# Lightning attention and an ELU expert on one core: block 1's keys and values in fp32 from another queue, one product of GpSimd moved, and fifteen products that nothing reads

## The chip, the core and the metric

The kernel runs on one core of a Trainium2 chip. The metric is the device time of one execution, in microseconds; 2% counts as a difference in the verdicts.

## The reference

Two stages, fp32 in and out.

Attention with decay, for 4 batches and 8 heads, 768 positions in 12 blocks of 64, head size 64. In each block, with a state per head that starts at zero:

```
intra = ((q k^T) * lam^(i-j), where i >= j) v
inter = (q * lam^(i+1)) state
out   = intra + inter
state = lam^64 * state + (k * lam^(63-j))^T v
```

The output, 3072 tokens of 512 features, then goes through `h = x @ w_in` (512 to 2048), `g = h if h > 0 else exp(h) - 1`, and `g @ w_out` (2048 to 512).

## The kernel before, in words

The four batches make two pairs; a "block" of the kernel is one block of 64 positions of both batches of a pair, 128 rows, so there are 24 of them (`NS`), numbered so that block 0 is the first of pair 0 and block 1 the first of pair 1. Two blocks make a group of 256 tokens (`grp`, 12 of them).

The order of the work is written out by hand: each engine executes its instructions in the order in which the program emits them. For the first blocks the order is the string `start`, of words such as `V1` (a letter for a step, a number for a block); the rest is a loop over groups and over eight units `u` of each.

The steps of a block: keys, queries and values are loaded and cast to fp16 (`load`, line 79; the queries of the first blocks at line 76) by GpSimd's DMA queue, which casts on the way. `visit(so, us, ss, sx)` (word `A`) is TensorE's work on up to four blocks: the output of block `so` (lines 337 and 346), the state product of `us` (353), the scores of `ss` (361), the transposes of `sx` (404 for queries, 409 for keys). Around it: `V` is `decay_v` (line 205, tile vd, the values scaled by the tile rev), `C` is `att_C` (251 and 252, the transposes copied out of PSUM into T), `P` the masked scores (240), `Q` is `decay_q` (232, tile qs, the queries scaled by powi), `D` is `decay_s` (223, tile sd, the decayed state), `N` the new state (293 and 297, tile st), `X` the copy of a block's output into xt (281). `K1` computes lamL and powi on ScalarE (608, 610); `F` casts block 0's fp32 keys and queries (193). From block 10 on the transposes come from a DMA (`dma_T`, tile TD), and `decay_q` runs on GpSimd.

The second stage: `H` is a unit of mm1 (line 434, PSUM tile psH, two buffers), `E` and `G` its ELU (444, 446 on ScalarE, 451 on VectorE; in the later loop 478, 480 and 481), `M` a part of mm2 (501), `Z` its copy and store (508, 510). In the loop mm2 is done as seven half-size products per group (557) on sums and differences `s` of parts of g (539) and `wt` of w_out.

The loads before the change, all on GpSimd's queue in this order: block 0's values, block 1's keys, queries and values, the first quarter of w_in (`wi[0]`, two transfers, line 97), block 2, `wi[1]`, block 3, `wi[2]`, `wo[0]` (a quarter of w_out, line 105), `wi[3]`, `wo[1]`, `wo[2]`, block 4, `wo[3]`, and so on. Block 0's keys come in fp32 on the sync queue SP (line 121), its queries in fp32 on ScalarE's queue (line 118). GpSimd has eight semaphores for its transfers, taken in turn: an issue waits until the transfer eight issues earlier has landed. In the loop, two loads of a later block are issued in units 0 and 4 of a group, and `decay_q` of the next block in unit 1 or 5.

Of the kernel before, what the change touches and what calls it, by code (L numbers as in the profile page):

```python
# [8 lines left out]
FP32 = mybir.dt.float32  # L9
FP16 = mybir.dt.float16  # L10
# [6 lines left out]
def kernel(  # L17
# [10 lines left out]
    nc = tc.nc  # L28

    B, H, S, D = q.shape  # L30
    L = 64
# [21 lines left out]
    def half(x):  # L53
        return slice(64 * x, 64 * x + 64)
# [5 lines left out]
    NB = 12  # L60
# [6 lines left out]
    def eights(b, c):  # L67

        return q[b : b + 2, :, c * L : (c + 1) * L, :].rearrange("r h (p g) d -> (r h) p (g d)", g=8)
# [14 lines left out]
    def load_step(s):  # L84
        load("k", s)
        load("q", s)
        load("v", s)
# [23 lines left out]
    for r in range(2):  # L111
        nc.gpsimd.iota(ij[half(r)], pattern=[[1, L]], base=0, channel_multiplier=-1)

    raw0 = {}
    for which, src in (("k", k), ("q", q)):
        raw0[which] = inp.tile([128, H, D], FP32, name=f"{which}raw0")
        if which == "q":
            nc.scalar.dma_start(out=raw0[which][:].rearrange("p h d -> p (h d)"), in_=eights(0, 0))
            continue
        for r in range(2):  # L120
            nc.sync.dma_start(
                out=raw0[which][half(r)], in_=src[r, :, 0:L, :].rearrange("h p d -> p h d")
            )
    load("v", 0)
    load_step(1)
    load_wi(0)
    load_step(2)
    load_wi(1)
# [60 lines left out]
    def cast0(which):  # L189

        keep, tag = {"k": (kn, "kn"), "q": (qn, "qn")}[which]
        keep[0] = inp.tile([128, H, D], FP16, tag=tag, bufs=NB, name=f"{tag}0")
        nc.vector.tensor_copy(keep[0][:], raw0[which][:])


    Z = ps.tile([128, 2, 512], FP32, tag="z", name="psZ")
    psS = Z[:, :, 0 : NHP * L]
# [3 lines left out]
    def decay_v(s, eng):  # L201
        if s >= NS - NPR:
            return
        st[s]["vd"] = asb.tile([128, H, D], FP16, tag="vd", bufs=3, name=f"vd{s}")
        eng.tensor_tensor(  # L205
            out=st[s]["vd"][:], in0=vn[s][:],
            in1=rev[:].unsqueeze(2).broadcast_to([128, H, D]), op=ALU.mult,
        )

# [32 lines left out]
            in1=mask[:].rearrange("p y j t -> p y (j t)"), op=ALU.mult,  # L242
        )

    def att_C(s):
        if s >= NT:
            return
        T = asb.tile([128, 2, NHP, 2, L], FP16, tag="T", bufs=4, name=f"T{s}")
        psT = st[s].pop("psT")
        if s < NQ:  # L250
            nc.vector.tensor_copy(T[:, 0].rearrange("p j r t -> p (j r t)"), psT[0])
            nc.scalar.copy(
                out=T[:, 1].rearrange("p j r (t g) -> p (j r t) g", g=8),
                in_=psT[1].rearrange("p (g x) -> p x g", g=8),
            )
        else:
            nc.vector.tensor_copy(
                T[:].rearrange("p i j r t -> p r (i j) t"),
                psT.rearrange("p r (x t) -> p r x t", t=L),
            )  # L260
        st[s]["T"] = T
# [12 lines left out]
    def att_X(s, eng):  # L274
        g, hf = divmod(s, 2)
        if g not in xt:
            xt[g] = asb.tile([128, NHP, 256], FP16, tag="xt", bufs=3, name=f"xt{g}")
        to = xt[g][:, :, hf * 128 : (hf + 1) * 128].rearrange("p y (r t) -> p r y t", r=2)
        O = st[s].pop("O").rearrange("p r (y t) -> p r y t", y=NHP)
        if eng is nc.scalar:  # L280
            nc.scalar.copy(out=to, in_=O)  # L281
        else:
            eng.tensor_copy(to, O)
# [134 lines left out]

    gel = {}
    unit = {}  # L420
    NF2 = NFT // 2

    def features(nb, n0, step):
# [79 lines left out]
                start=(n == 0), stop=(n == NFT - 1),  # L503
            )

    def mm2_o(s):
        o = msb.tile([128, DM], FP32, tag="o", bufs=4, name=f"o{s}")
        nc.scalar.copy(out=o[:], in_=acc.pop(s))
        for r in range(2):
            nc.sync.dma_start(out=rows(s, r), in_=o[half(r), :])  # L510

# [89 lines left out]
    def consts(i):  # L601
# [10 lines left out]


    start = (
# [14 lines left out]
    steps = {  # L629
        "C": att_C, "P": att_P, "X": lambda s: att_X(s, nc.scalar),  # L630
        "Y": lambda s: att_X(s, nc.vector), "N": att_N, "D": lambda s: decay_s(s, eng=nc.vector), "L": load_step,
        "V": lambda s: decay_v(s, nc.vector if s < 99 else nc.gpsimd),
        "Q": lambda s: decay_q(s, nc.vector if s < 10 else nc.gpsimd),
        "H": mm1_h, "E": mm1_e, "G": mm1_g, "M": mm2, "Z": mm2_o, "K": consts, "B": w_sum, "T": dma_T,
    }
    for word in start.split():
        if word[0] == "A":
            visit(*(int(x) if x else None for x in word[1:].split(".")))
        elif word[0] == "F":
            cast0(word[1])  # L640
        else:
            steps[word[0]](*(int(x) for x in word[1:].split(".") if x))

# [6 lines left out]
    for grp in range(3, NG):  # L650
        old, new = grp - 2, grp - 1
        for u in range(8):
            mm1_h(grp, 0, 2, u, NF2)
            s = 2 * grp + 2 + u // 4
            if s < NS and u % 4 == 0:

                if nload < NS:
                    load("k", nload)
                    load("q", nload)
                if nload <= NS:  # L660
                    load("v", nload - 1)
                    nload += 1
            if s < NS and u % 4 == 1:
                if s != 10:
                    decay_q(s + 1, nc.vector if s < 10 else nc.gpsimd)
                if s not in (10, 11, 12):
                    decay_s(s + 1, eng=nc.vector if s < 10 else nc.gpsimd)
                visit(
                    s, s if s < NS - NPR else None, s + 1 if s + 1 < NS else None,
                    s + 2 if s + 2 < NT else None,  # L670
                )
                dma_T(s + 3)

            if (grp, u) in five:
                mm2(5, 4 * five.index((grp, u)))
            end = grp == NG - 1
            if old >= 3 and u in (0, 2):
                part(old, {0: 3, 2: 7}[u])
            if new >= 3:
                at_u = {1: 2, 3: 4, 4: 1, 5: 5, 6: 6, 7: 3} if end else {3: 2, 4: 1, 5: 4, 6: 5, 7: 6}  # L680
                if u in at_u:
                    part(new, at_u[u])

            if old >= 3 and u == 1:
                add(old, 0, hi, res[old]["A"][:, hi], "p35")
                store(2 * old, res[old][0], slice(0, DM))
            if old >= 3 and u == 0:
                g_sum(old, 3)
            if new >= 3 and u in (4, 5, 6):
                g_sum(new, {4: 1, 5: 2, 6: 4}[u])  # L690
            if end and u == 3:
                g_sum(new, 3)
            if new >= 3 and u == 4:
                add(new, 0, lo, res[new]["A"][:, hi], "p2")
            if s + 1 < NS:
                if u % 4 == 1:
                    att_P(s + 1)
                if u % 4 == 2:
                    att_C(s + 2)
                    att_N(s)  # L700
                if u in (3, 7) and grp > 3:
                    decay_v(s + 1, nc.vector)
                if (grp, u) == (4, 2):
                    decay_q(s + 1, nc.vector)
            if old >= 3 and u == 2:
                c2(old)
            if (grp, u) == (5, 0):
                w_sum(3, 1)
            elu(grp, u)
            if (grp, u) == (4, 4):  # L710
                decay_s(11)
            if (grp, u) in ((5, 2), (5, 4)):
                decay_s(13, range(2) if u == 2 else range(2, NHP))
            if grp == 3 and u in (3, 6):
                decay_v(s + 1, nc.vector)
            if s < NS and u % 4 == 1:
                att_X(s, nc.scalar)
            if (grp, u) == (4, 5):
                decay_s(12)
            if old >= 3 and u == 0:  # L720
                keep(old, "p35", res[old]["B"][:, hi])
            if new >= 3 and u == (1 if end else 3):
                keep(new, "p2", res[new]["B"][:, lo])
            if new >= 3 and u == (5 if end else 6):
                keep(new, "c45", res[new]["B"][:])
            if end and u == 6:
                keep(new, "u2", res[new]["A"][:, hi], 1)
            if end and u == 7:
                add(new, 0, hi, res[new]["B"][:, hi], "u2")
                store(2 * new, res[new][0], slice(0, DM))  # L730
            if (grp, u) == five[-1]:
                mm2_o(5)
# [58 lines left out]
```

## Time and profile before

| | |
|---|---|
| three runs | 206.19, 206.64, 209.43 us; median 206.64 |
| the profiled execution | 207.57 us |
| its span, first to last instruction | 205.8 us |
| ScalarE (ACT) busy | 146.4 us |
| GpSimd (POOL) busy, its DMA issues included | 122.4 us |
| DMA | 94258 packets, 24.36 MB |
| issues of keys by GpSimd (kn, x46) | 64.0 KB each, 4.5 us to landing |
| issues of w_in (wi, x8) | 256.0 KB each, 6.5 us to landing |

PE is TensorE, PEld its weight loads, DVE VectorE, ACT ScalarE, POOL GpSimd, SP the sync queue. In a line of the timeline stand the start and the length in us, engine, line of the kernel, operation, tiles written and read, shapes and count; in brackets the idle time of the engine ahead of it and what the profile holds to have ended it. In the page's rows of slices each digit is the busy share of a fortieth of the span in tenths. The DMA rows give packets, MB, and the time that the packets took as a share of 16 engines' time (packets overlap, so it can pass 100%).

### The profile page before, as it was taken

Reading aid. Unit: us, or ns where it says so; the run is one execution under the profiler, and the core shown is the slowest. Engines: PE = TensorE matmul, PEld = TensorE weight load, DVE = VectorE, ACT = ScalarE, POOL = GpSimd, SP = SyncE. Lnnn points to the kernel's source line nnn. Section 1 sums busy time; section 2 is a strip of 40 time slices with the busy share of each in tenths; the row PEclk is TensorE's granted clock in tenths of the full one; section 3 lists DMA queues with packets and bytes.
Section 4 is the critical chain, followed back from the end, with each engine's and each line's share of the span. In section 5 each row is a group of like instructions: output and inputs, shape, how many; then the busy total and the mean of one; then the engine's idle time right before and its main releaser. Section 6 shows DMA issues by size and latency. Waiting matters only on the chain.

```text
span 205.8 us, 7718 instructions
## 1 busy us (share of the span) xinstructions
PE 190.1 (92%) x3280; PEld 158.0 (77%) x3280; DVE 165.9 (81%) x278; ACT 146.4 (71%) x283; POOL 122.4 (59%) x173
## 2 busy tenths in 40 slices
PE   0679799999999999989999999999999999999991
PEld 0457678747776777878888888888888888888880
DVE  4677786779989898999988988979979866658671
ACT  5435786834783888997978878788688788876720
POOL 8986642899799779796978978978222200000000
PEclk9999999999999999999999999999999999999999
DMA  6999999999999999999799999999814204003043
GB/s 102 164 170 173 166 206 190 177 115 175 108 136 160 163 126 130 155 110 128 108 152 108 169 103 118 156 102 127 137 25 102 54 5 102 5 21 84 0 102 102
DMA packets 94258, 24.36 MB, mean 118 GB/s; under 512 B 86160, under 2 KB 91152, under 8 KB 94224
## 3 DMA queue, kind: packets, MB, share of 16 engines
q0 software_dynamic: 73648, 13.38, 92.6%
q1 hardware_dynamic: 20128, 10.03, 27.8%
q10 hardware_dynamic: 448, 0.46, 1.0%
q8 instruction: 25, 0.41, 0.9%
q14 instruction: 9, 0.07, 0.1%
HBM read 27.27 MB, written 6.29 MB: 163 GB/s over the span
## 4 chain that ended last, share of the span: by engine, by line
PE 85%; DVE 5%; POOL 3%; DMA 3%; issue 1%; ACT 1%; DVEq 0%; POOLq 0%; ACTq 0%
PE psH L434 40%; PE psM L557 22%; PE psM L501 10%; DMA wi<-in_moe_w_in_dram 3%; PE psO_None L337 2%; PE psZ L361 2%; POOL vn L79 1%; PE psO_None L346 1%; PE psHB L557 1%; PE psHA L557 1%; DVE g L451 1%; PE psZ L353 1%; DVE s L539 1%; DVE vd L205 1%; POOL kn L79 1%
## 5 line engine op out<-in xcount | busy, mean ns | idle before, releaser
L434 PE MATMUL psH<-xt,wi 128*128 128x256 f16 (+1 forms) x960 | 100.3, 254 | 2.7 <-issue 1.0
L434 PEld LDWEIGHTS <-wi 128*128 128x128 f16 x960 | 79.5, 99 | 13.3 <-issue 2.5
L481 DVE SCALAR_TENSOR_TENSOR g<-e,psH 128x512 f16<-128x512 f32 x58 | 39.8, 686 | 16.7 <-ACT e L480 16.2
L478 ACT ACTIVATE r<-psH 128x512 f32<-128x512 f32 x58 | 34.7, 599 | 18.3 <-PE psH L434 18.2
L480 ACT ACTIVATE e<-r 128x512 f32<-128x512 f32 x58 | 36.5, 630 | 1.9
L79 POOL DMA_DIRECT2D kn<-in_k_dram x46 | 32.3, 723 | 6.7 <-DMA wo<-in_moe_w_out_dram 3.6
L79 POOL DMA_DIRECT2D vn<-in_v_dram x48 | 33.8, 731 | 3.5 <-DMA wo<-in_moe_w_out_dram 2.0
L444 ACT ACTIVATE e<-psH 128x512 f32<-128x512 f32 x38 | 22.8, 599 | 16.3 <-PE psH L434 15.8
L557 PEld LDWEIGHTS <-s 128*128 128x128 f16 x288 | 28.1, 98 | 3.3
L451 DVE SCALAR_TENSOR_TENSOR g<-e,r 128x512 f16<-128x512 f32 x38 | 25.9, 687 | 4.9 <-ACT r L446 4.8
L79 POOL DMA_DIRECT2D qn<-in_q_dram x36 | 25.4, 736 | 1.4 <-DMA kn<-in_k_dram 0.9
L557 PE MATMUL psM<-wt,s 128*128 128x256 f16 x192 | 24.9, 273 | 0.0
L501 PE MATMUL psM<-wo,g 128*128 128x512 f16 x96 | 23.9, 379 | 0.0
L232 POOL TENSOR_TENSOR qs<-TD,powi 128x512 f16<-128x512 f16 x12 | 14.6, 1215 | 15.4 <-PE psO_None L337 13.7
L446 ACT ACTIVATE r<-psH 128x512 f16<-128x512 f32 x38 | 22.7, 598 | 0.0
L557 PEld LDWEIGHTS <-g 128*128 128x128 f16 x216 | 20.6, 98 | 2.6
L240 DVE TENSOR_TENSOR P<-psZ,mask 128x512 f16<-128x512 f32 x24 | 16.5, 687 | 1.8 <-PE psZ L361 1.4
L557 PE MATMUL psM<-wo,g 128*128 128x256 f16 x136 | 17.6, 273 | 0.0
L205 DVE TENSOR_TENSOR vd<-vn,rev 128x512 f16<-128x512 f16 x22 | 16.0, 729 | 0.1
L293 DVE TENSOR_TENSOR st<-psZ,sd 128x512 f16<-128x512 f32 x20 | 13.7, 684 | 1.0 <-PE psZ L353 0.9
L501 PEld LDWEIGHTS <-g 128*128 128x128 f16 x96 | 8.6, 98 | 7.1
L281 ACT CAST xt<-psO_None 128x512 f16<-128x512 f32 x20 | 11.6, 579 | 3.1 <-PE psO_None L346 3.1
(84 smaller groups left out, 214.1 us busy)
## 6 DMA issues: line engine op xcount, KB each, us to landing
out_dram<-o SPq DMA_DIRECT2D x45, 128.0 KB, 3.6
vn<-in_v_dram POOLq DMA_DIRECT2D x48, 64.0 KB, 5.0
kn<-in_k_dram POOLq DMA_DIRECT2D x46, 64.0 KB, 4.5
qn<-in_q_dram POOLq DMA_DIRECT2D x36, 64.0 KB, 4.4
wi<-in_moe_w_in_dram POOLq DMA_DIRECT2D x8, 256.0 KB, 6.5
wo<-in_moe_w_out_dram POOLq DMA_DIRECT2D x4, 512.0 KB, 11.7
qn<-in_q_dram POOLq DMA_DIRECT2D x5, 128.0 KB, 5.5
kraw<-in_k_dram SPq DMA_DIRECT2D x2, 128.0 KB, 4.8
```

Source lines behind the costliest of these rows:

```text
L79: nc.gpsimd.dma_start(out=keep[s][half(r)], in_=src[b + r, :, c * L : (c + 1) * L, :].rearrange("h p d -> p h d"),)
L205: eng.tensor_tensor(out=st[s]["vd"][:], in0=vn[s][:], in1=rev[:].unsqueeze(2).broadcast_to([128, H, D]), op=ALU.mult,)
L240: nc.vector.tensor_tensor(out=d["P"][:].rearrange("p y j t -> p y (j t)"), in0=psS, in1=mask[:].rearrange("p y j t -> p y (j t)"), op=ALU. ...
L434: nc.tensor.matmul(psH[:, i, :], lhsT=wi[n // 4][:, kk, (n % 4) * 128 : (n % 4 + 1) * 128], rhs=xt[grp][:, kk, c0 * 128 : c0 * 128 + T], s ...
L444: nc.scalar.activation(e[:], psH[:], AF.Exp)
L446: nc.scalar.activation(r[:], psH[:], AF.Relu)
L451: nc.vector.scalar_tensor_tensor(out=place(grp, c0, nc_, n0, nb, step), in0=e[:], scalar=-1.0, in1=r[:], op0=ALU.add, op1=ALU.min,)
L478: nc.scalar.activation(r[:], psH[:], AF.Relu, scale=-1.0)
L480: nc.scalar.activation(e[:], r[:], AF.Exp, scale=-1.0)
L481: nc.vector.scalar_tensor_tensor(out=place(grp, 0, 2, u, 2, NF2), in0=e[:], scalar=-1.0, in1=psH[:], op0=ALU.add, op1=ALU.max,)
L501: nc.tensor.matmul(acc[s], lhsT=g_of(s, n), rhs=wo[n // 4][:, n % 4, :], start=(n == 0), stop=(n == NFT - 1),)
L557: nc.tensor.matmul(to, lhsT=lhsT, rhs=rhs, start=start and n == 0, stop=stop and n == NF2 - 1, skip_group_check=True,)
```

## The change

Three edits.

1. Block 1's keys and values are no longer loaded by GpSimd. They come in fp32 over the sync queue, behind block 0's keys, and ScalarE casts them to fp16 (`cast1`, words `fk` and `fv`). Block 1's decayed values are computed from the fp32 tile.
2. In the loop, `decay_q` of block 13 is emitted in group 5's unit 4, between the loads of block 17's keys and queries, and no longer in unit 1 of that group, which precedes both.
3. A step `U` issues products of the identity with four copies of itself into a psH buffer that nothing reads: eight ahead of all else, one ahead of block 0's state product, three while P of block 0 is made, one ahead of block 1's state product, two ahead of the first mm1 unit.

The other lines (a `copy` argument of `att_C` and `mm2_o`, steps `c`, `d`, `z`) are not used by any word of the order.

```
-    raw0 = {}
-    for which, src in (("k", k), ("q", q)):
-        raw0[which] = inp.tile([128, H, D], FP32, name=f"{which}raw0")
+    raw0, raw1 = {}, {}
+    for s, which, src in ((0, "k", k), (0, "q", q), (1, "k", k), (1, "v", v)):
+        raw = (raw1 if s else raw0)[which] = inp.tile([128, H, D], FP32, name=f"{which}raw{s}")
...
             nc.sync.dma_start(
-                out=raw0[which][half(r)], in_=src[r, :, 0:L, :].rearrange("h p d -> p h d")
+                out=raw[half(r)], in_=src[2 * s + r, :, 0:L, :].rearrange("h p d -> p h d")
             )
     load("v", 0)
-    load_step(1)
+    load("q", 1)
...
+    def cast1(which):
+        keep, tag = {"k": (kn, "kn"), "v": (vn, "vn")}[which]
+        keep[1] = inp.tile([128, H, D], FP16, tag=tag, bufs=NB, name=f"{tag}1")
+        nc.scalar.copy(out=keep[1][:], in_=raw1[which][:])
...
-            out=st[s]["vd"][:], in0=vn[s][:],
+            out=st[s]["vd"][:], in0=raw1["v"][:] if s == 1 else vn[s][:],
...
+    def unread(n):
+        to = ps.tile([128, 4, 128], FP32, tag="h", bufs=2, name="psU")
+        for i in range(n):
+            nc.tensor.matmul(
+                to[:], lhsT=ident[:], rhs=ident[:].unsqueeze(1).broadcast_to([128, 4, 128]),
+                start=True, stop=True,
+            )
...
-        "Fq Fk V0 A...0 C0 A.0.. K1 N0 A...1 K0 A..0. P0 V1 A0... X0 D2 A.1.. N1 H0.0.1.0 C1 D3 "
+        "U8 Fq Fk V0 A...0 C0 U1 A.0.. fk K1 N0 A...1 K0 A..0. P0 U3 fv V1 A0... X0 D2 U1 A.1.. N1 U2 H0.0.1.0 C1 D3 "
...
                 if nload < NS:
                     load("k", nload)
+                    if (grp, u) == (5, 4):
+                        decay_q(s, nc.gpsimd)
                     load("q", nload)
...
-                if s != 10:
+                if s not in (10, 12):
                     decay_q(s + 1, nc.vector if s < 10 else nc.gpsimd)
```

More of the change, by code (lines that the diff above doesn't have):

```diff
@@ L112 @@
         nc.gpsimd.iota(ij[half(r)], pattern=[[1, L]], base=0, channel_multiplier=-1)
-    raw0 = {}
-    for which, src in (("k", k), ("q", q)):
-        raw0[which] = inp.tile([128, H, D], FP32, name=f"{which}raw0")
+    raw0, raw1 = {}, {}
+    for s, which, src in ((0, "k", k), (0, "q", q), (1, "k", k), (1, "v", v)):
+        raw = (raw1 if s else raw0)[which] = inp.tile([128, H, D], FP32, name=f"{which}raw{s}")
         if which == "q":
-            nc.scalar.dma_start(out=raw0[which][:].rearrange("p h d -> p (h d)"), in_=eights(0, 0))
+            nc.scalar.dma_start(out=raw[:].rearrange("p h d -> p (h d)"), in_=eights(0, 0))
             continue
@@ L243, in att_P, with att_C @@
         )
-    def att_C(s):
+    def att_C(s, copy=nc.scalar.copy):
         if s >= NT:
@@ L251, in att_C @@
             nc.vector.tensor_copy(T[:, 0].rearrange("p j r t -> p (j r t)"), psT[0])
-            nc.scalar.copy(
-                out=T[:, 1].rearrange("p j r (t g) -> p (j r t) g", g=8),
-                in_=psT[1].rearrange("p (g x) -> p x g", g=8),
+            copy(
+                T[:, 1].rearrange("p j r (t g) -> p (j r t) g", g=8),
+                psT[1].rearrange("p (g x) -> p x g", g=8),
             )
@@ L504, in mm2, with mm2_o @@
             )
-    def mm2_o(s):
+    def mm2_o(s, copy=nc.scalar.copy):
         o = msb.tile([128, DM], FP32, tag="o", bufs=4, name=f"o{s}")
-        nc.scalar.copy(out=o[:], in_=acc.pop(s))
+        copy(o[:], acc.pop(s))
         for r in range(2):
@@ L631 @@
         "Y": lambda s: att_X(s, nc.vector), "N": att_N, "D": lambda s: decay_s(s, eng=nc.vector), "L": load_step,
+        "c": lambda s: att_C(s, nc.vector.tensor_copy), "d": decay_s,
+        "z": lambda s: mm2_o(s, nc.vector.tensor_copy),
         "V": lambda s: decay_v(s, nc.vector if s < 99 else nc.gpsimd),
@@ L634 @@
         "H": mm1_h, "E": mm1_e, "G": mm1_g, "M": mm2, "Z": mm2_o, "K": consts, "B": w_sum, "T": dma_T,
+        "U": unread,
     }
@@ L640 @@
             cast0(word[1])
+        elif word[0] == "f":
+            cast1(word[1])
         else:
```

## The prediction

> **What bounds the kernel now.** I read the page first, then TensorE's timeline of the first 30 us, GpSimd's issues beside it, the waits, the DMA view in short windows, and last a close look at 88 to 93 us, where TensorE idles in an otherwise full stretch.
>
> ```profile
> span 205.8 us, 7718 instructions
> PE 190.1 (92%) x3280; PEld 158.0 (77%) x3280; DVE 165.9 (81%) x278; ACT 146.4 (71%) x283; POOL 122.4 (59%) x173
> PE   0679799999999999989999999999999999999991
> q0 software_dynamic: 73648, 13.38, 92.6%
> ```
>
> TensorE is the bound: 190.1 of 205.8 us, and full in nearly every slice after the sixth. Its 15.7 us of idle time are the first 6.45, about 4 between 6.45 and 30, one hole at 91, and 4.5 at the tail. The change works on the front and, with block 13, on the hole.
>
> ```profile
> 6.45 0.64 PE L404 MATMUL psM<-ident,qn 128*64 128x64 f16 x16 [6.45 <-DVE qn L193]
> ...
> 12.64 1.89 PE L434 MATMUL psH<-xt,wi 128*128 128x128 f16 x16 [0.50 <-DMA wi<-in_moe_w_in_dram]
> ...
> 17.05 1.87 PE L434 MATMUL psH<-xt,wi 128*128 128x128 f16 x16
> ...
> 19.61 2.01 PE L434 MATMUL psH<-xt,wi 128*128 128x128 f16 x32
> ...
> 25.48 1.24 PE L434 MATMUL psH<-xt,wi 128*128 128x128 f16 x19 [1.01 <-issue]
> ```
>
> The timeline of GpSimd:
>
> ```profile
> 17.71 0.62 POOL L97 DMA_DIRECT2D wi<-in_moe_w_in_dram  x1 [0.96 <-DMA wi<-in_moe_w_in_dram]
> 25.56 0.54 POOL L76 DMA_DIRECT2D qn<-in_q_dram  x1 [1.67 <-DMA wi<-in_moe_w_in_dram]
> ```
>
> Two things are to be seen. Sixteen products of one form take 1.89 us at 12.64 and 1.87 at 17.05, but 32 take 2.01 at 19.61: TensorE runs at half rate until about 19 us (the granted clock in the page reads full all along, so only the durations show it). And the wait of 1.01 us ahead of 25.48, labelled "issue", stands at the first product that reads the third quarter of w_in (wi[2]); the second half of wi[2] was issued at 17.71 and the DMA view gives it 7.6 us to landing, 25.3, and GpSimd's issue that waits for the same landing goes at 25.56. So at 25.5 the load stream sets the pace, whatever TensorE did before.
>
> ```profile
> 89.27 1.32 POOL L232 TENSOR_TENSOR qs<-TD,powi 128x512 f16<-128x512 f16 x1
> ...
> 89.48 1.65 DVE L539 TENSOR_TENSOR s<-g,s 128x1024 f16<-128x1024 f16 x1
> 91.06 0.68 DVE L293 TENSOR_TENSOR st<-psZ,sd 128x512 f16<-128x512 f32 x1
> 91.66 0.67 DVE L481 SCALAR_TENSOR_TENSOR g<-e,psH 128x512 f16<-128x512 f32 x1
> ...
> 92.38 1.03 PE L434 MATMUL psH<-xt,wi 128*128 128x256 f16 x8 [0.76 <-DVE g L481]
> ```
>
> The hole: VectorE's sum s takes 1.65 us, where the same form takes 0.68 at 93.45. It began while GpSimd was computing block 13's decayed queries (qs, 89.27 to 90.59) and ended 0.55 after those. (The same pair stood at 84: vd, 83.97, took 1.65 beside block 12's qs, 83.74 to 85.08; g and P beside such a qs kept their 0.68 to 0.69.) The g behind it frees the PSUM buffer for which TensorE stood from 91.35 to 92.38.
>
> **The change part by part.** *Block 13's queries.* The instruction moves behind the two issues of block 17's keys (1.41 us), so from 89.27 to about 90.6, ending near 91.9; those issues go 1.3 earlier, block 17's queries and block 16's values keep their places (the same three rows in another order). Its reader, block 13's visit, runs at 102.0 and has 10 us of cover; without that cover the move would cost 1.3. The sum s then takes 0.68 (89.48 to 90.16), the state add to 90.76, and g, whose e is ready at 90.74, ends at 91.44. TensorE goes on at 91.49 in place of 92.38: a gain of 0.9. The next two-input fp16 operation, vd (92.25 in the trace, then 91.4), meets qs instead and ends near 92.4; the g behind it ends at 93.1, when TensorE, at 93.2 by then, first needs it. Bounds: 0 gain if qs slides on to the wrong operation again, 1.03 if the hole closes. I take 0.9.
>
> *The loads.* Four issues (1.37 and 1.40 us) leave GpSimd's queue; wi[0] goes out at 3.4 in place of 6.08. On SP four issues follow the first two (0.62 to 0.76 each, to about 5 us); behind them SP has nothing until its first store at 43.84. Whether wi[2] lands sooner hangs on the DMA engines, which are busy in that stretch. Three windows of the DMA view price a packet of 256 B from a hardware queue (q1) beside the software queue (q0), the first from 75 to 77, the second from 74 to 75, the third from 5 to 6 us:
>
> ```profile
> q0 software_dynamic: 2416, 0.30, 239.5%
> ...
> q0 software_dynamic: 509, 0.06, 100.0%
> q1 hardware_dynamic: 525, 0.13, 79.4%
> ...
> q0 software_dynamic: 674, 0.08, 156.1%
> q1 hardware_dynamic: 296, 0.07, 55.3%
> ```
>
> Alone, q0 moves 1208 packets per us, so block 1's 2048 packets on it cost 1.7 us. On SP they are again 2048 packets. By the second window they cost (1 - 509/1208)/525 = 1.10 ns each, 2.25 us; by the third (1 - 674/1208)/296 = 1.49 ns, 3.05 us; at the far end stands the first 512 packets' own rate when nothing else ran (212 in 0.5 us from 2.3), 2.36 ns, 4.8 us; at the other, nothing, if they ride in gaps. So wi[2] would land between 1.7 sooner and 3.1 later. I take the second window, the one with both queues backlogged (0.55 later), less the gaps of the stream that a second queue can fill: from 8 to 13 us, 1969 small packets at 1208 per us and 612 large at 200 per us (597 in the 3 us from 25) make 4.7 of 5 us, 0.3 free; from 19 to 25, 423 small and 886 large make 4.8 of 6, 1.2 free. I count 0.5 of these 1.5: net 0.
>
> *The two casts and the late arrival.* Block 0's keys land at 7.1 (1.55 and 5.5 to landing). Behind them, at 525 packets per us, block 1's keys land near 9.1 and its values at 11.0; at 296 per us, 10.5 and 14.0. I take 9.6 and 12.3. Each cast on ScalarE is 0.6 (its copies of 128x512 are 0.59 to 0.62); behind the first waits the lamL and powi work (1.26 us, wanted by VectorE only from 11.6), behind the second the first xt. First mm1 products: 12.3 + 0.6 cast + 0.59 xt + 0.2 of handing over = 13.7, in place of 12.64: 1.1 later. On VectorE vd of block 1 waits for the same landing, with sd, the new state and T of block 1 behind it, all wanted by work after that mm1 group. The decayed values read fp32 now: 0.69 as for sd, against 0.68.
>
> *The fifteen products.* At half rate one of 512 columns takes about four of 128, 0.118 x 4 = 0.47; at full rate 1.03/4, some 0.22 to 0.26. Eight stand ahead of the first transposes: from 1.5 (ident) to 5.3, hidden by the wait until 6.45. One delays the state product by 0.47, hidden by the wait for block 1's keys. Three fit between the scores and P (0.8 us at 11.1) at full rate and stick out by 0.6 at half. The last three lie in the wait for vd and xt. If the clock rises early, two mm1 groups save 0.9 each and seven small groups about 0.1 each: 2.5. I take half, 1.2.
>
> TensorE then reaches the wi[2] products at 24.46 + 1.1 - 1.2 = 24.4, still 1.0 ahead of the landing. Cost of all this: nothing, the wait at 25.48 hides it; with that cover gone it would be the difference itself.
>
> **Sum.** 0 at the front, -0.9 at the hole. On the profiled execution (span 205.8, 1.8 around it, 207.57) that is 206.7; its time stands 0.9 above the median of the runs, 206.64, to which I apply the difference: 205.7 us.
>
> **The rivals.** *The front gains* (0.25). The 256 B packets ride in gaps and wi[2] lands 1.7 sooner, 23.6; TensorE with the full 2.5 us of faster clock reaches it at 23.1. Time 206.64 - 0.9 - 1.7 = 204.0. For it: in 19 to 25 the stream moves 1308 packets, 1.2 us less than it could. Against: at 5 to 6 both queues together move 970 packets where q0 alone has 1208.
>
> *The clock carries all the way* (0.05). If wi[2] came from a stream that keeps up, the front would gain the wait of 1.0 and the 2.5 of the clock, and 206.64 - 0.9 - 3.5 = 202.2. Against: the landing at 25.3. The Trainium skill, TensorE: Matmul & The Clock Gate, Part 1, says that the array runs at half clock until a window of some 3.4 us has been busy, and falls back after an idle one; by that rule the eight early products nearly fill a window and the later ones keep the gate from falling, so the clock would be full long before 19 us. The trace agrees on the step, at 19 us, and shows nothing of an earlier one.
>
> *Slower at the front* (0.20). The one mechanism: a 256 B packet of the sync queue costs more engine time than one of 128 B cast on the way. At the third window's 1.49 ns and with no gaps filled, wi[2] lands 1.35 later; at the lone rate, 3.1. In the middle, 2.2 later: 206.64 + 2.2 - 0.9 = 207.9. It decides the sign from 0.9 later on, that is from 1.27 ns per packet if no gap is filled, 1.51 if 0.5 us are.
>
> *The hole stays* (0.10). The change would not do what it says there if qs meets another two-input fp16 operation ahead of the g that TensorE needs: vd is the next, and it stands one g too late for that. Time 206.6.
>
> **How the numbers follow.** The forecast, 205.7, has 0.40, the rivals 0.25, 0.05, 0.20 and 0.10. The range leaves out about one in ten at either side: from just under the front's gain, 203.9, to just over the packets' price, 208.2. Its own range, front within 0.6 either way, is 205.1 to 206.3. Two per cent are 4.1 us, about what a measurement of this kernel can tell from no change (its three runs lie 3.2 apart). Under 202.5 lies the carried clock: 0.06. Over 210.8 lies the lone packet rate (208.8) with a late arrival on top: 0.04. Within: 0.90.
>
> **What would show it.** The hole at 91: s at 0.7 us and no idle time ahead of the mm1 group there. The front: the wait ahead of the first wi[2] product, still there and ending near 25.5; the first mm1 group at about 13.7 and near 1 us long; the casts waiting for their transfers; the landing of the second half of wi[2] near 25.3. Wrong would make it: that wait gone, or values of block 1 landing after 15 us, when TensorE becomes the later one.

## The result, and the profile after

The kernel after takes 209.02 us (median of four runs, 208.49 to 210.25); the kernel before, with one more run beside these, 207.9 (206.19 to 209.43). Some executions of a kernel are slow ones, before's longest among them, so the ratio is taken over the fast runs alone: 1.0118, 95% interval 1.0073 to 1.0163. That is slower by 1.2%, some 2.4 us, and within the 2% of the verdicts. The forecast was 205.7 in a range of 203.9 to 208.2. So the sign is wrong, and the time lies above the range.

The page of the profiled execution after (208.49 us, 1.9 of them outside the span):

```profile
span 206.5 us, 7753 instructions
PE 194.5 (94%) x3295; PEld 158.6 (77%) x3295; DVE 165.5 (80%) x278; ACT 147.6 (71%) x285; POOL 119.8 (58%) x169
PE   6468999999999999999999999999999999999991
```

TensorE has 4.4 us more work; the unread products fill the first slice, but the next three are emptier than before (4, 6, 8 in place of 6, 7, 9). The 8 in the 18th slice, the hole at 91 us, is gone. TensorE's timeline after:

```profile
1.58 3.29 PE L433 MATMUL psU<-ident 128*128 128x512 f16 x8 [1.58 <-DVE ident L154]
...
12.27 0.61 PE L416 MATMUL psM<-ident,kn 128*128 128x128 f16 x4 [2.34 <-ACT kn L200]
...
13.16 1.46 PE L433 MATMUL psU<-ident 128*128 128x512 f16 x3
...
15.82 1.04 PE L433 MATMUL psU<-ident 128*128 128x512 f16 x2
16.65 1.74 PE L450 MATMUL psH<-xt,wi 128*128 128x128 f16 x16
...
20.53 1.05 PE L450 MATMUL psH<-xt,wi 128*128 128x128 f16 x16 [0.17 <-ACT xt L288]
...
26.23 1.96 PE L450 MATMUL psH<-xt,wi 128*128 128x128 f16 x32
```

The first unit of mm1 starts at 16.65, where it stood at 12.64: 4.0 later, not 1.1. The unit that first reads wi[2] is the second half of the group at 26.23; its first product starts at 27.1, against 25.65 before; no wait stands ahead of it. At 12.27 TensorE waits 2.34 us for block 1's keys. ScalarE says what these wait for:

```profile
11.59 0.62 ACT L200 CAST kn<-kraw 128x512 f16<-128x512 f32 x1 [4.13 <-DMA kraw<-in_k_dram]
...
14.46 0.62 ACT L200 CAST vn<-vraw 128x512 f16<-128x512 f32 x1 [1.19 <-DMA vraw<-in_v_dram]
```

Both casts stand waiting for their transfers, as forecast, but the keys land at 11.5 and the values at 14.4, where I had 9.6 and 12.3. The DMA view of after shows why; the first rows are those from 5 to 6 us, the second those from 8 to 11:

```profile
q0 software_dynamic: 500, 0.06, 111.9%
q1 hardware_dynamic: 399, 0.10, 73.0%
...
q0 software_dynamic: 461, 0.42, 89.6%
q1 hardware_dynamic: 529, 0.13, 35.0%
```

From 5 to 6 us the software queue moves small packets (0.06 MB in 500), and the sync queue gets 399 through. From 8 to 11 the software queue moves w_in (0.42 MB in 461, most of 1024 B written), and the sync queue gets 529 in three microseconds, 176 per us. The counts of the two queues stay near each other while w_in's packets take some 2.6 times as long (by the shares, 0.093 us in place of 0.036). So block 1's packets crawl as soon as wi[0] runs, and the change had just moved wi[0] 2.7 us forward, beside them.

The Trainium skill, DMA: Bandwidth & Descriptors, section Queues, rings and completion order, says that a DMA engine serves the queues that have work for it in turn, a packet each. The rows above agree in their counts; how many records of the trace make one such turn they don't show.

At 91 us, VectorE after:

```profile
91.09 0.68 DVE L555 TENSOR_TENSOR s<-g,s 128x1024 f16<-128x1024 f16 x1
...
92.97 1.33 DVE L212 TENSOR_TENSOR vd<-vn,rev 128x512 f16<-128x512 f16 x1
```

The sum keeps its 0.68 us, and vd meets the moved product (GpSimd, 92.59 to 93.75), as the prediction had it; no idle time of TensorE is left there. In these two executions the front costs 1.5 us (27.1 against 25.65) and the hole gives 0.8 back, and the spans differ by 0.7. The runs without a profile lie further apart (2.4), so the hole can't be counted on; the experiments below look into it.

### The profile page after: what moved, and what is told of

Its sections match the earlier page's. It is cut to its first block, busy times and chain, and to the rows that moved or that the text cites. A ratio compares the mean times of both kernels' runs of the same rounds, so it can differ in the third digit from the quotient of the medians.

```text
span 206.5 us, 7753 instructions
## 1 busy us (share of the span) xinstructions
PE 194.5 (94%) x3295; PEld 158.6 (77%) x3295; DVE 165.5 (80%) x278; ACT 147.6 (71%) x285; POOL 119.8 (58%) x169
## 4 chain that ended last, share of the span: by engine, by line
PE 83%; DVE 7%; DMA 4%; ACT 2%; SPq 1%; issue 1%; DVEq 0%; ACTq 0%
PE psH L450 38%; PE psM L573 22%; PE psM L517 10%; DMA kraw<-in_k_dram 4%; PE psO_None L344 2%; PE psZ L368 1%; PE psU L433 1%; PE psZ L360 1%; DVE vd L212 1%; PE psHA L573 1%; PE psHB L573 1%; DVE g L467 1%; PE psO_None L353 1%; DVE s L555 1%; SPq L122 1%
## 5 line engine op out<-in xcount | busy, mean ns | idle before, releaser
L450 PE MATMUL psH<-xt,wi 128*128 128x256 f16 (+1 forms) x960 | 99.2, 253 | 0.5 <-ACT r L462 0.3
L79 POOL DMA_DIRECT2D vn<-in_v_dram x46 | 32.6, 732 | 6.6 <-DMA wo<-in_moe_w_out_dram 2.3
L79 POOL DMA_DIRECT2D kn<-in_k_dram x44 | 30.9, 724 | 5.3 <-DMA wo<-in_moe_w_out_dram 3.6
L460 ACT ACTIVATE e<-psH 128x512 f32<-128x512 f32 x38 | 22.8, 599 | 14.8 <-PE psH L450 14.4
L467 DVE SCALAR_TENSOR_TENSOR g<-e,r 128x512 f16<-128x512 f32 x38 | 25.7, 686 | 4.2 <-ACT r L462 4.1
L300 DVE TENSOR_TENSOR st<-psZ,sd 128x512 f16<-128x512 f32 x20 | 13.7, 683 | 0.0
L230 POOL TENSOR_TENSOR sd<-st,lamL 128x512 f32<-128x512 f16 x8 | 8.3, 1039 | 8.5 <-DVE st L300 8.5
```

What stands on the lines that cost most here:

```text
L79: nc.gpsimd.dma_start(out=keep[s][half(r)], in_=src[b + r, :, c * L : (c + 1) * L, :].rearrange("h p d -> p h d"),)
L450: nc.tensor.matmul(psH[:, i, :], lhsT=wi[n // 4][:, kk, (n % 4) * 128 : (n % 4 + 1) * 128], rhs=xt[grp][:, kk, c0 * 128 : c0 * 128 + T], s ...
L460: nc.scalar.activation(e[:], psH[:], AF.Exp)
L467: nc.vector.scalar_tensor_tensor(out=place(grp, c0, nc_, n0, nb, step), in0=e[:], scalar=-1.0, in1=r[:], op0=ALU.add, op1=ALU.min,)
```

## The experiments

All ratios are to before, over five rounds, but for one kernel that ran once; "first unit" is the start of the first mm1 unit in the one profiled execution (12.64 in before's; the two other kernels whose front is that of before have 12.42 and 12.85, so it is good to some 0.2 us).

**One part alone.** Edit 2 of the change by itself, edit 1 (with the two casts), edit 3, and after without edit 3. The queries alone:

```
                     load("k", nload)
+                    if (grp, u) == (5, 4):
+                        decay_q(s, nc.gpsimd)
                     load("q", nload)
...
-                if s != 10:
+                if s not in (10, 12):
```

> The kernel before with one part of the change: block 13's decayed queries between the loads of block 17. Theory A (the hole at 91 us was GpSimd holding up VectorE's sum, and nothing takes its place): 0.9 us faster than before, ratio about 0.996, the sum s near 0.7 us and TensorE's hole of 1.03 us closed. Rival (the time comes back later, in another wait): hole closed, ratio 1.000.

The loads alone (the word string has `fk` and `fv`, and no `U`):

```
+    for s, which, src in ((0, "k", k), (0, "q", q), (1, "k", k), (1, "v", v)):
...
-    load_step(1)
+    load("q", 1)
```

> The kernel before with block 1's keys and values on the sync queue and their casts alone, no unread products, block 13's queries at the old place. Theory A (the late landing of block 1 is the loss): keys land near 11.5, values near 14.4 us, the first mm1 group starts near 15.7 in place of 12.64, the wait for wi[2] is gone, and the kernel is 0.8 to 1.7 us slower, ratio 1.004 to 1.008. Theory B (the unread products are the loss): the wait for wi[2], which in the changed kernel lands 1.15 us sooner, still covers the late start: ratio 0.995 to 1.000.

The products alone:

```
-        "Fq Fk V0 A...0 C0 A.0.. K1 N0 A...1 K0 A..0. P0 V1 A0... X0 D2 A.1.. N1 H0.0.1.0 C1 D3 "
+        "U8 Fq Fk V0 A...0 C0 U1 A.0.. K1 N0 A...1 K0 A..0. P0 U3 V1 A0... X0 D2 U1 A.1.. N1 U2 H0.0.1.0 C1 D3 "
```

> The kernel before with the fifteen unread products alone. Theory A: the first mm1 group starts about 1 us late (three products of 0.43 behind the scores, three more ahead of that group), which the 1.0 us of waiting for wi[2] at 25.5 absorbs: ratio 0.998 to 1.002; the clock rises near 4.5 us, falls near 8 and rises again at 15 to 19. Theory B: 1.5 us slower, ratio 1.007. If the clock stayed up: first mm1 group near 1 us long, and still no gain, since wi[2] lands at 25.3.

After without the products (against after):

```
-        "U8 Fq Fk V0 A...0 C0 U1 A.0.. fk K1 N0 A...1 K0 A..0. P0 U3 fv V1 A0... X0 D2 U1 A.1.. N1 U2 H0.0.1.0 C1 D3 "
+        "Fq Fk V0 A...0 C0 A.0.. fk K1 N0 A...1 K0 A..0. P0 fv V1 A0... X0 D2 A.1.. N1 H0.0.1.0 C1 D3 "
```

> The changed kernel without the fifteen unread products: both other parts stay. Theory A: the first mm1 group starts near 15.7 rather than 16.65 and the clock rises at its own time (18 to 19 us): 0.3 to 0.9 us faster than the changed kernel, ratio to before 0.999 to 1.005. Theory B (products are the whole loss): 1.6 us faster than the changed kernel, ratio 0.996. If the products had earned something through the clock: slower than the changed kernel, ratio above 1.005.

| kernel | ratio | 95% interval | first unit |
|---|---|---|---|
| queries alone | 0.9966 | 0.9917 to 1.0016 | 12.85 |
| loads alone | 1.0109 | 1.0065 to 1.0153 | 14.92 |
| products alone | 0.9976 | 0.9942 to 1.0010 | 13.22 |
| after, no products | 1.0131 | 1.0078 to 1.0185 | 15.36 |

The loads alone give the whole loss, and neither of the other two parts changes it by more than the intervals. The expectations had the loads alone at 1.004 to 1.008 and after without products at 0.999 to 1.005; both came out slower. The products alone move the time by -0.5 us (-1.2 to +0.2). The hole was not removed by the move of the queries: in the profiled execution of that kernel (208.57 us, above its median of 207.38) the moved product ran from 90.05 to 91.57 and met two operations, and TensorE idled 1.55 us for the g behind them, more than in before. VectorE, and below it TensorE, of the queries alone:

```profile
89.10 1.45 DVE L451 SCALAR_TENSOR_TENSOR g<-e,r 128x512 f16<-128x512 f32 x1
90.47 1.65 DVE L539 TENSOR_TENSOR s<-g,s 128x1024 f16<-128x1024 f16 x1
```

```profile
93.37 1.03 PE L434 MATMUL psH<-xt,wi 128*128 128x256 f16 x8 [1.55 <-DVE g L481]
```

The g of line 451 reads two SBUF tiles, like s, and is long as well; with its usual 0.68 it would have ended 0.27 us ahead of the product's recorded start, so that the product held it is likely (the times of GpSimd are rough) and not shown. Which operation the product meets is set by where VectorE stands when GpSimd gets there, to a few tenths of a microsecond; with the loads alone, where the product has its old place, no idle time came at 91 either.

**What makes block 1 late.** The keys alone on the sync queue, the values back on GpSimd's; wi[0] behind block 2; the values on ScalarE's queue; and GpSimd held until the values are there. All are the loads alone with one difference, and the last is not meant to be fast. Keys only:

```
-    for s, which, src in ((0, "k", k), (0, "q", q), (1, "k", k), (1, "v", v)):
+    for s, which, src in ((0, "k", k), (0, "q", q), (1, "k", k)):
...
     load("q", 1)
+    load("v", 1)
     load_wi(0)
```

> Only block 1's keys go over the sync queue; its values stay on GpSimd's queue, in 128 B packets ahead of wi[0]; no products, block 13's queries where they were. Theory (packets of the sync queue alternate one for one with whatever the software queue has in flight, so the 1024 small fp32 packets of a tensor cost the time of as many packets of wi[0] once wi[0] runs): keys land near 10 to 11, because the 1024 packets of the values run ahead of wi[0]'s; values land near 8.5; first mm1 unit near 13.5, half of the delay that both loads together gave (12.6 to 14.9); ratio to before 1.000 to 1.006. Rival (it is the number of bytes or of issues on the sync queue that makes the front late, whatever runs beside it): half the bytes, and the keys land near 11.3 as with both loads; then the first mm1 unit, which the keys of block 1 hold up through the scores, is as late as with both, near 14.5, ratio 1.009.

w_in later:

```
     load("q", 1)
-    load_wi(0)
     load_step(2)
+    load_wi(0)
```

> Both loads on the sync queue, no products, block 13's queries where they were, but wi[0] is issued behind block 2's loads, so that block 1's fp32 packets run beside 128 B packets and not beside w_in's. Theory (one-for-one alternation with long packets is the cause): block 1's values land about 2 us sooner than in the kernel with the loads alone (13.7), near 11.5 to 12; wi[0] lands near 13 and then ends the wait ahead of the first mm1 unit; block 1's scores and state stand where they stood in before or earlier; ratio between 0.998 and 1.005. Rival (the price is that of a 256 B packet, whatever it runs beside): values land at 13.5 to 14 as before, first mm1 unit near 15, ratio 1.010.

Two queues:

```
-            nc.sync.dma_start(
+            (nc.scalar if which == "v" else nc.sync).dma_start(
```

> Both loads in fp32, keys on the sync queue and values on ScalarE's queue behind block 0's queries, so three queues run side by side; wi[0] stays early; no products, block 13's queries where they were. Theory (each queue with packets waiting gets one packet in turn, whatever their lengths): two hardware queues get two turns to wi[0]'s one, values and keys land together near 11 to 11.5, values 2 us sooner than on the one queue (13.7), wi[0] some 1.5 later (12.5 to 13.5); first mm1 unit near 13.5, ratio 1.002 to 1.006. Rival (the hardware queues share one turn, or the price is the packet's own): values land at 13.5 to 14 as on one queue, ratio 1.010.

GpSimd held:

```
     load("q", 1)
+    seen = inp.tile([128, H, 1], FP32, name="seen")
+    nc.gpsimd.tensor_copy(out=seen[:], in_=raw1["v"][:, :, 0:1])
     load_wi(0)
```

> The kernel with the two loads alone, but GpSimd reads a column of block 1's values ahead of wi[0], so that nothing runs on the software queue from block 1's queries until those values have landed; not meant to be fast. Theory (the fp32 packets are late because they alternate with w_in's): keys land near 9 and values near 10.5, 3 us sooner than with wi[0] beside them (13.7). Rival (it is the packet's own price): values land at 13 to 14 all the same.

| kernel | keys, values landed | first unit | ratio | 95% interval |
|---|---|---|---|---|
| loads alone | 11.3, 13.7 | 14.92 | 1.0109 | 1.0065 to 1.0153 |
| keys only | 9.6, 10.5 | 13.28 | 1.0017 | 0.9978 to 1.0056 |
| w_in later | 9.9, 12.9 | 16.17 | 1.0153 | 1.0100 to 1.0205 |
| two queues | 12.2, 10.6 | 15.85 | 1.0131 | 1.0084 to 1.0178 |
| GpSimd held | 9.7, 11.0 | 18.43 | 1.024 | one run |

The packets of the DMA view settle the mechanism better than the landings do. Loads alone, 8 to 11 us:

```profile
q0 software_dynamic: 483, 0.45, 92.3%
q1 hardware_dynamic: 498, 0.12, 30.6%
```

w_in later, the same three microseconds:

```profile
q0 software_dynamic: 1245, 0.27, 111.6%
q1 hardware_dynamic: 1043, 0.26, 63.9%
```

GpSimd held, 8 to 10 us:

```profile
q1 hardware_dynamic: 1163, 0.29, 122.8%
q0 software_dynamic: 1, 0.00, 0.0%
```

The same packets of the sync queue go at 166 per us beside w_in, 348 beside mostly small packets and 582 alone. That excludes a price of the packet's own. The expected landings were hit only in part: w_in later brought the values 0.8 us sooner, not 2 (from 10 to 12 us some 100 packets of wi[0] already ran beside the last of them); on two queues the values came 3.1 sooner but the keys 0.9 later, and TensorE needs the keys first. In both the first unit got later still (in "w_in later" it waits 1.98 us for wi[0]; in "two queues" TensorE waits 2.41 for the keys), so neither paid: 1.0153 and 1.0131, where 0.998 to 1.005 and 1.002 to 1.006 were expected. By the 2% of the verdicts "w_in later" is unclear, and every other kernel with an interval the same as before.

First unit and ratio together answer the question of cover. Without the products, a first unit 0.64, 2.28, 2.72 (after without products), 3.21, 3.53 and 5.79 us later than before's costs 0.4, 2.3, 2.7, 2.7, 3.2 and 5.0 us (the ratio less one, times 206.6). So far as one execution tells a kernel's lateness, nearly every microsecond of it reaches the end; the wait of 1.0 us that was to swallow it swallows nothing over the runs.

**Where the cover went.** In the timeline of "two queues" the wait of before stands again:

```profile
28.08 1.22 PE L450 MATMUL psH<-xt,wi 128*128 128x128 f16 x19 [1.24 <-issue]
```

and its wi[2], issued at 16.78 and 17.39, had landed by 23.8 (the DMA view's median is 6.1 us):

```profile
wi<-in_moe_w_in_dram POOLq DMA_DIRECT2D x2, 256.0 KB, 6.1
```

So wi[2] is not what TensorE waits for. Counted from the first product, the wait stands ahead of number 349 (counting from 0) in before, here, in the loads alone (0.29), in after without products (0.52), in w_in later (0.35) and with GpSimd held (0.29). Number 349 is in the middle of a unit that reads wi[1]; wi[2] is first read three products on, at 352. In a kernel with the fifteen products all later work moves up by fifteen numbers, and the wait, where there is one, stays at 349: "products, wi[2] ahead" (below) has 0.45 there, and "together" (below) the line that follows, both in the middle of a group of scores, which reads nothing of w_in:

```profile
24.56 0.22 PE L371 MATMUL psZ<-T 64*64 64x64 f16 x2 [1.11 <-issue]
```

The queries alone have the wait too, though a short one. The rows of the products run over it; that of the weight loads shows it:

```profile
25.32 1.12 PEld L434 LDWEIGHTS <-wi 128*128 128x128 f16 x20 [0.25 <-issue]
```

Some 1.3 to 1.6 us before each of these waits ends, a packet of 16 KB ends on a queue that the page names "instruction"; this is the DMA view of "two queues" from 25.5 to 25.7 us:

```profile
q8 instruction: 1, 0.02, 27.9%
```

All fourteen traces have this packet, and the wait goes with it. Where it starts when TensorE has begun 276 to 295 products (after, products alone, queries later, products with queries later), product 349 is not late. Where it starts at 304 or 305 (queries alone, keys only), 349 comes 0.1 to 0.2 us late (start to start from 348, less the usual 0.06); at 307 to 314 it is 0.5 to 0.7, at 320 to 325 (before, two queues, together) 1.2 to 1.4. In time these places lie between 22.7 and 31.4 us. So the wait goes with TensorE's own progress and not with the landing of a load: a TensorE that comes later meets it later, and it can't absorb lateness. The label "issue" says only that the profile shows nothing that was waited for. That TensorE's instructions come with this packet, and came late, is the likeliest reading and was not tried by itself; what sets the packet's start is open.

**Towards a version that beats both.** wi[2] ahead of block 3's values, with the products; the queries made behind block 14's, beside operations that read PSUM; that with the products; and all of it with the keys alone on the sync queue. Products, wi[2] ahead (against the products alone):

```
-    load_step(3)
+    load("k", 3)
+    load("q", 3)
     load_wi(2)
+    load("v", 3)
```

> A version meant to be faster than both: loads as before, but wi[2] is issued ahead of block 3's values (one issue and 64 KB earlier), and the fifteen products that nothing reads are in. Theory (with the products alone the wait of 0.9 us for wi[2] stayed, and was what was left between the clock's gain and the span): wi[2] lands 0.7 to 0.9 sooner, the wait at its first product falls to 0.2 or less, ratio to before 0.992 to 0.996. Rival (the wait only moves on, to block 3's values or to wo[0] behind it): ratio 0.997 to 1.000, as with the products alone.

Queries later:

```
-                if s != 10:
+                if s not in (10, 12):
                     decay_q(s + 1, nc.vector if s < 10 else nc.gpsimd)
+                if s == 13:
+                    decay_q(s, nc.gpsimd)
```

> Before, with one difference: block 13's decayed queries are made behind block 14's, some 8 us later, where VectorE runs only operations that read PSUM. Theory (the hole at 91 us is VectorE's operation on two SBUF tiles held up by this GpSimd product, and the new place of the change only moved the collision in some executions): s at about 89.5 keeps 0.68 us, every operation of VectorE beside the moved product keeps 0.7, no idle time of TensorE over 0.3 us between 87 and 102; ratio 0.994 to 0.997. Rival (the hole has another cause, such as the landing of the transposes for block 13, and comes back): TensorE idles 0.6 to 1.5 us there as before, ratio 0.999 to 1.001.

The next is this edit and the products, the last this edit, the products, wi[2] ahead and keys only.

> All loads as in before; the fifteen products and block 13's queries behind block 14's. Theory: the products' gain (0.9976 alone) and that of the hole (0.995) add, 0.991 to 0.994. Rival (the hole is not tied to that product): 0.997 to 0.999.

> A version meant to beat both: block 1's keys alone over the sync queue (its values in 128 B packets ahead of wi[0]), the fifteen products, wi[2] issued ahead of block 3's values, and block 13's queries behind block 14's. Theory (the three gains add, since each takes away what limits the next): first mm1 unit near 13.3 at half its length, wi[2] landing near 22.7 and no wait ahead of its first product, no hole; ratio 0.980 to 0.988. Rival (the front is set by the load stream as a whole, and a wait only moves to the next transfer): TensorE waits about a microsecond for block 3's values or the first quarter of w_out; ratio 0.992 to 0.996.

| kernel | ratio | 95% interval | first unit |
|---|---|---|---|
| products, wi[2] ahead | 0.9973 | 0.9935 to 1.0011 | 12.93 |
| queries later | 0.9999 | 0.9955 to 1.0043 | 12.42 |
| products, queries later | 0.9968 | 0.9927 to 1.0008 | 12.98 |
| together | 0.9972 | 0.9949 to 0.9994 | 14.48 |

With the queries later the hole is gone, and s keeps its time:

```profile
88.50 0.68 DVE L539 TENSOR_TENSOR s<-g,s 128x1024 f16<-128x1024 f16 x1
```

yet the ratio is 0.9999. In the products alone TensorE waits 0.72 us at 24.00, at number 367, fifteen after 352: this wait goes with the work. The profile names ScalarE's e as its end; "products, queries later" waits as long at the same number, and there wi[2] lands at 24.12 and the product starts at 24.21, so the wait on wi[2] is real where TensorE comes that early. "Products, wi[2] ahead" has wi[2] at 22.7 and no wait at 367, but 0.45 us at 349, and its time is that of the products alone. None of the four reached the ratio that its theory named. "Together" missed its 0.980 to 0.988: its first unit is 1.8 later than before's, since the products, most of them at half rate, stand in line with block 1's late keys, and the wait at number 349 took another 1.1. It is the only kernel whose interval lies below one, by less than 0.1%; its ratio is that of the products alone, and among eleven intervals one so close is no proof that it beats before.

## Why the prediction was wrong

Put the measured terms into the prediction's own sum. With 4.0 in place of 1.1, TensorE reaches the wi[2] products at 24.46 + 4.0 - 1.2 = 27.3, 2.0 past the landing at 25.3, and the whole is 2.0 - 0.9 = 1.1 slower: this term alone turns the sign. Without the cover the front costs 2.8 and the whole 1.9; without the gain at the hole it is 2.8. Measured were 2.4 us (1.5 to 3.4 by the interval).

*"I take 9.6 and 12.3 ... 1.1 later."* This is the step that failed first, and the one that turns the sign. The term was mis-sized: 4.0, more than three times as much. The landings account for 2.1 (14.4 against 12.3). They were priced at rows in which the software queue moved packets of 128 B (296 to 525 per us), while the change itself put w_in's beside them (176). Even the slower of these rows gave 10.5 and 14.0, short of the measured 11.5 and 14.4. A bound that holds could have been had by counting turns: in the rows of w_in alone that the prediction used (200 per us), a queue that gets one packet for each of those gets 200 at most. The two products ahead of the first unit took another 0.8: xt was ready at 15.6 and the unit began at 16.65, so they didn't lie "in the wait for vd and xt".

*"Cost of all this: nothing, the wait at 25.48 hides it."* This is the second step that failed. The prediction took the wait ahead of product 349 for the wait on wi[2], because the landing (25.3) and GpSimd's next issue (25.56) fell within 0.3 us of it. They did so in one execution. The label said "issue", not DMA, and the group had broken after 13 products of a unit of 16; both spoke against it in lines that I showed. In that execution wi[2] would have held TensorE too, from 24.5 to 25.3. In the queries alone, whose front is that of before, 0.25 us stand there, and in queries later nothing. In the pair of profiles the wait still hid a part, since after has none: 2.65 us late (below) became 1.5. Over the runs lateness was paid in full.

*"I take half, 1.2"* for the clock: from 4.0 late at the first unit TensorE was 2.65 late at number 352 (27.1 against 24.46, before's without its wait), so 1.35 came back in this pair. But after without products stands at 1.0131 beside 1.0118, and the products alone save 0.5 us, neither clear of the intervals: over the runs the 1.2 is not to be seen. The granted clock in the profile after, and behind it a row of the products alone (columns: the stretch and its length, busy time of each engine, then PEclk, the DMA share and GB/s; ahead of its first change PEclk reads full though the products run at half rate):

```profile
5.00:10.00 5.00, 2.39 (x53) 1.61 (x53) 2.48 (x5) 1.56 (x6) 3.72 (x6) 0.78 1.42 180
10.00:15.00 5.00, 2.73 (x40) 1.30 (x40) 1.91 (x4) 2.22 (x7) 2.13 (x4) 0.50 1.59 174
15.00:20.00 5.00, 4.66 (x87) 3.34 (x88) 3.50 (x7) 2.69 (x7) 2.97 (x5) 0.69 1.64 187
...
10.00:15.00 5.00, 5.00 (x105) 2.86 (x104) 3.98 (x8) 1.76 (x4) 4.16 (x7) 0.75 1.64 175
```

The eight early products do raise the clock (0.44 us for the transposes at 6.39 in place of 0.64), and it falls again, to 0.50 from 10 to 15 us, and is up for good only at 18 us. In the products alone, with block 1 on time, it falls as well, but not for so long: 0.75 from 10 to 15, full from 15 on. That block 1's lateness prolongs the half clock, since it leaves TensorE 2.73 us of work in those five in place of 5.00, is likely and was not tried by itself.

*The loads themselves, "net 0"*: right in that the stream got no later. wi[2] landed at 24.1, 1.2 sooner than before; it was worth nothing, since TensorE was not there.

*"A gain of 0.9"* at the hole: the mechanism is shown (a GpSimd product holds up VectorE's operations on two SBUF tiles, 0.68 becoming 1.33 to 1.65), the gain is not. The move as made doesn't remove the collision in every execution, and the kernel that did remove it came to 0.9999, whose interval just reaches 0.9 us. Why a hole of 0.8 us in the trace leaves no mark on the median is not settled; of the eight profiled kernels with the product at its old place, five have the hole (0.54 to 1.14 us) and three do not, so before's profile may have shown an unlucky one.

Of the rivals, *slower at the front* had the sign and was given 0.20. Its mechanism, a sync-queue packet that costs more beside another queue, is near the truth; its path was not: wi[2] came sooner, and the price was paid at block 1. The line "Wrong would make it ... values of block 1 landing after 15 us" set the point too late by the very cover that wasn't there.

## What to carry to other kernels

A wait labelled "issue" that breaks a group at an odd count is not the wait of the tile that the next group reads: count the products, and see in another kernel whether the wait stays with the work or with the number. A load moved to a second queue is to be priced against what will run beside it after the move, not against what runs there now: with long packets in the other queue, many short ones get as few turns as the long ones. And a cover seen in a single execution, ended by two things within 0.3 us, is not a cover to subtract.

## What the runs showed of the hardware

The step of TensorE's clock does not come at a fixed time. With the same work ahead of it, the second mm1 unit took 1.87 us at 17.05 in before and, in queries later:

```profile
16.49 1.05 PE L434 MATMUL psH<-xt,wi 128*128 128x128 f16 x16
```

The queries alone, with the same front too, passes number 352 at 25.5, 0.25 us of it the wait at 349, and queries later at 24.0. The trace's record of the granted clock puts the step at 18.8 us in before, at 20.7 in the queries alone and at 15.1 in queries later. The spans of the runs of before that the ratios use lie between 203.0 and 207.1. The Trainium skill, TensorE: Matmul & The Clock Gate, Part 1, says that the window in which activity is judged runs freely and isn't reset by the kernel; the executions named here agree. One profile against another can't price an edit in this front below some 1.5 us.
